# Cutting one weight load into 112, 8 and 8 partitions, so that the first eight DMA engines carry two rows more than the last eight

## The chip, the cores and the metric

The kernel runs on one core of one Trainium2 chip. Times are device microseconds of one execution; the shorter the better. A profiled execution gives a span (first to last instruction), about 1.8 us shorter than the time of the same run. Each run carries a state, slow when it took over 1.5% more than the fastest run of the same kernel.

## The reference, cut to what matters

Attention over pooled keys and values (batch 8, 8 heads, 576 positions, 64 dimensions) gives `x` of 4608 x 512. A soft mixture of 8 experts follows, 4 slots for each: 32 slots are weighted sums of all rows of `x`, each expert runs two dense layers on its slots, and each row of the output is a weighted sum of all slots.

```python
logits = x @ phi
d = exp(logits - logits.max(0)); d /= d.sum(0) + 1e-09
slot_input = (d.T @ x).reshape(E, S_per_e, D)
for e in range(E):
    h = np.maximum(slot_input[e] @ w1[e], 0.0)     # w1[e]: 512 x 1024 float32
    slot_out[e] = h @ w2[e]                        # w2[e]: 1024 x 512 float32
c = exp(logits - logits.max(1)); c /= c.sum(1) + 1e-09
return c @ slot_out
```

The inputs are 62 MB of float32 and the output 9.4 MB. The slots need all rows of `x`, and the output needs all slots.

## The kernel before

All inputs except `phi` are loaded by GpSimd (POOL), whose transfers convert float32 to bfloat16 on the way: first q, k and v in four pairs of batches, then `w1` of the eight experts, then `w2`. Each of these transfers covers 128 partitions. The last `w2` loads are cut by columns, so that the first half of the output columns can start before the rest has landed.

```python
    w1_sb = persist.tile([128, E, DJ, F], BF)

    def load_w1(e):
        nc.gpsimd.dma_start(out=w1_sb[:, e], in_=moe_w1[e].rearrange("(p j) f -> p j f", j=DJ))
    ...
    for pair in range(1, NP):
        ...                                   # k, q and v of the pair
        if pair == NP - 2:
            load_w1(0)
    for e in range(1, E):
        load_w1(e)
    load_w2(range(4), big, "big")
    ...
    for c in range(2):
        second(E - 2, c)                      # matmuls of expert 6 on column half c
        if c == 0:
            warm(6, junk)                     # filler matmuls that keep PE's clock up
        second(E - 1, c)                      # expert 7: waits for the last weights of half c
        slots_out(c)
        for g in range(NHALF):
            output(g, halves[c])
```

The softmax here doesn't subtract the row's maximum and nothing guards it: scores larger than these inputs give would overflow.

## Time and profile before

| | before |
|---|---|
| time, median of the first 6 runs | 178.92 us (177.95 to 179.39) |
| span of the profiled run | 176.2 us (time 178.02) |
| DMA queue 0 (all loads but `phi`), share of 16 engines | 86.6% |
| last weights of the first column half land | 146.76 us |
| last output lands | 174.56 us |

The page's table of 40 slices (each 4.4 us) has these rows for DMA; a digit is a tenth of the 16 engines' time, and below it stand the GB/s:

```profile
DMA  4999999999999999999999999999999999999995
GB/s 71 211 220 209 221 211 213 221 213 219 211 220 215 217 213 219 213 210 218 221 214 210 218 219 216 212 218 216 216 212 216 206 196 146 316 362 423 419 417 208
```

The engines are at least 90% busy from the second slice to the last but one. The loads count by what they write (bfloat16), so 215 GB/s written is 430 GB/s read. The queues of the same page (packets, MB, share of the engines' time):

```profile
q0 software_dynamic: 6768, 30.93, 86.6%
q1 hardware_dynamic: 3872, 9.50, 13.9%
q8 instruction: 11, 0.18, 0.4%
q14 instruction: 3, 0.02, 0.0%
```

Queue 1 carries the output and `phi`. Queue 8: eleven packets of 16 KB with instructions, 0.4% of the engines.

The chain of waits in order of time (start us, length us, what) around the end of the loads:

```profile
76.68 39.03 DMA w_big<-in_moe_w_dram
...
116.28 30.48 DMA w_xs<-in_moe_w_dram
146.76 0.04 issue
146.81 0.43 PE so_ps_2181 L447 x8
```

And PE's own timeline of these microseconds (start, length, what; in brackets how long it was idle before, and for what):

```profile
141.44 2.79 PE L112 MATMUL junk<-zeros 128*128 128x512 bf16 x7 [0.33 <-issue]
144.16 0.40 PE L447 MATMUL so_ps_2181<-w_xs,hT 128*32 128x256 bf16 x8
144.49 1.47 PE L112 MATMUL junk<-zeros 128*128 128x512 bf16 x6
146.81 0.40 PE L447 MATMUL so_ps_2181<-w_xs,hT 128*32 128x256 bf16 x8 [0.84 <-DMA w_xs<-in_moe_w_dram]
```

PE is done with everything else, fillers included, 0.84 us before the last weights come. The landing at 146.76 starts the outputs, and those are limited by DMA as well: 1 MB each 2.5 us to the end. So what moves this landing should move the time.

A landing is the sixteenth and last of the DMA engines' reports. The trace has all 16 times of each load. For the load that PE waits for here they are, in us behind the first of them (worked out from the trace's records, as all plain fences below):

```
0.00 0.18 0.35 0.38 0.58 0.70 0.85 1.11 1.24 1.33 1.40 1.61 2.03 2.54 2.55 2.64
```

The first engine was through 2.64 us before the last, and on average they were through 1.42 us before it: that is what a perfect balance could win here.

### The profile page before, as it was taken

Reading aid. Unit: us, or ns where it says so; the run is one execution under the profiler, and the core shown is the slowest. Engines: PE = TensorE matmul, PEld = TensorE weight load, DVE = VectorE, ACT = ScalarE, POOL = GpSimd, SP = SyncE. Lnnn points to the kernel's source line nnn. Section 1 sums busy time; section 2 is a strip of 40 time slices with the busy share of each in tenths; the row PEclk is TensorE's granted clock in tenths of the full one; section 3 lists DMA queues with packets and bytes.
Section 4 is the critical chain, followed back from the end, with each engine's and each line's share of the span. In section 5 each row is a group of like instructions: output and inputs, shape, how many; then the busy total and the mean of one; then the engine's idle time right before and its main releaser. Section 6 shows DMA issues by size and latency. Waiting matters only on the chain.

```text
span 176.2 us, 3523 instructions
## 1 busy us (share of the span) xinstructions
PE 134.0 (76%) x1467; PEld 84.2 (48%) x1469; DVE 90.7 (51%) x252; ACT 79.8 (45%) x146; POOL 18.5 (11%) x37
## 2 busy tenths in 40 slices
PE   7993999899999999999999869997422295787000
PEld 2363478557866678656755536356211132322000
DVE  5402602577777878778787696436000004899000
ACT  3022359697946978469798401120000003799000
POOL 6000100121001610111111001121200000000000
PEclk9999579999999999999999965999555569999655
DMA  4999999999999999999999999999999999999995
GB/s 71 211 220 209 221 211 213 221 213 219 211 220 215 217 213 219 213 210 218 221 214 210 218 219 216 212 218 216 216 212 216 206 196 146 316 362 423 419 417 208
DMA packets 10654, 40.64 MB, mean 231 GB/s; under 512 B 784, under 2 KB 6288, under 8 KB 6544
## 3 DMA queue, kind: packets, MB, share of 16 engines
q0 software_dynamic: 6768, 30.93, 86.6%
q1 hardware_dynamic: 3872, 9.50, 13.9%
q8 instruction: 11, 0.18, 0.4%
q14 instruction: 3, 0.02, 0.0%
HBM read 61.93 MB, written 9.44 MB: 405 GB/s over the span
## 4 chain that ended last, share of the span: by engine, by line
DMA 68%; PE 15%; ACT 6%; issue 2%; DVE 1%; POOL 0%; POOLq 0%; DVEq 0%
DMA w_big<-in_moe_w_dram 22%; DMA q_sb<-in_q_dram 18%; DMA w_xs<-in_moe_w_dram 17%; DMA v_sb<-in_v_dram 11%; PE f_ps L462 3%; PE q_ps L193 3%; PE pool_ps L179 3%; ACT w_sb L464 2%; PE sc L248 2%; PE G_ps L277 1%; PE u_ps L260 1%; PE fold_ps L204 1%; ACT ex_332 L249 1%; PE lg_ps L271 1%; DVE so L451 1%
## 5 line engine op out<-in xcount | busy, mean ns | idle before, releaser
L266 DVE TENSOR_TENSOR xs<-u_ps,rec 128x384 bf16<-128x384 f32 x72 | 39.4, 552 | 1.6
L248 PE MATMUL sc<-qT,kp 64*72 64x288 bf16 x128 | 22.9, 308 | 0.8 <-ACT ex_1633 L249 0.4
L265 DVE RECIPROCAL rec<-u_ps 128x4 f32<-128x4 f32 x72 | 12.5, 176 | 16.4 <-PE u_ps L260 16.1
L199 DVE COPY qT<-q_ps 128x768 bf16<-128x768 bf16 x16 | 8.8, 552 | 14.7 <-PE q_ps L193 14.6
L193 PE MATMUL q_ps<-ident,q_sb 128*128 128x128 bf16 x144 | 12.2, 229 | 4.4 <-DMA q_sb<-in_q_dram 3.9
L462 PE MATMUL f_ps<-so,cT 128*128 128x512 bf16 (+1 forms) x46 | 11.0, 331 | 3.5 <-DVE so L451 1.2
L464 ACT ACTIVATE o_sb_2311<-f_ps,recR 128x256 f32<-128x256 f32 x1 | 0.5, 474 | 29.1 <-PE f_ps L462 29.1
L451 DVE TENSOR_SCALAR so<-so_ps_2181,recC 128x256 bf16<-128x256 f32 x1 | 0.5, 484 | 23.9 <-PE so_ps_2181 L447 23.9
L248 PEld LDWEIGHTS <-kp 64*72 64x72 bf16 x128 | 8.7, 107 | 8.0 <-issue 2.5
L193 PEld LDWEIGHTS <-q_sb 128*128 128x128 bf16 x144 | 9.1, 102 | 6.4 <-DMA q_sb<-in_q_dram 4.8
L447 PEld LDWEIGHTS <-hT 128*32 128x32 bf16 x128 | 4.2, 118 | 16.4 <-issue 15.8
L112 PEld LDWEIGHTS <-zeros 128*128 128x128 bf16 x51 | 5.7, 119 | 9.8 <-issue 6.1
L182 ACT CAST kpar<-pool_ps 128x512 bf16<-128x512 f32 (+1 forms) x12 | 5.5, 485 | 10.6 <-PE pool_ps L179 10.5
L197 ACT COPY qT<-q_ps 128x768 bf16<-128x768 bf16 x8 | 6.4, 797 | 8.6 <-PE q_ps L193 8.6
L179 PE MATMUL pool_ps<-pmat,v_sb 128*128 128x128 bf16 x144 | 10.2, 227 | 0.0
L277 PE MATMUL G_ps<-xs,ee 128*128 128x512 bf16 x36 | 9.7, 405 | 0.4 <-ACT ee L272 0.4
L179 PE MATMUL pool_ps<-pmat,k_sb 128*128 128x128 bf16 x144 | 9.7, 219 | 0.1
L179 PEld LDWEIGHTS <-v_sb 128*128 128x128 bf16 x144 | 8.8, 102 | 0.8 <-issue 0.2
L462 PEld LDWEIGHTS <-cT 128*128 128x128 bf16 x46 | 4.3, 96 | 10.0 <-issue 7.6
L179 PEld LDWEIGHTS <-k_sb 128*128 128x128 bf16 x144 | 8.5, 98 | 0.8 <-issue 0.2
L466 DVE TENSOR_SCALAR w_sb<-f_ps,recR 128x512 f32<-128x512 f32 x12 | 8.3, 746 | 0.0
L464 ACT ACTIVATE w_sb<-f_ps,recR 128x512 f32<-128x512 f32 x12 | 7.7, 684 | 0.6
(165 smaller groups left out, 236.9 us busy)
## 6 DMA issues: line engine op xcount, KB each, us to landing
w_sb<-in_moe_w_dram POOLq DMA_DIRECT2D x8, 1024.0 KB, 34.6
out_dram<-w_sb SPq DMA_DIRECT2D x6, 1024.0 KB, 8.5
k_sb<-in_k_dram POOLq DMA_DIRECT2D x4, 1152.0 KB, 19.8
q_sb<-in_q_dram POOLq DMA_DIRECT2D x4, 1152.0 KB, 18.3
v_sb<-in_v_dram POOLq DMA_DIRECT2D x4, 1152.0 KB, 18.1
w_big<-in_moe_w_dram POOLq DMA_DIRECT2D x4, 1024.0 KB, 39.0
w_qT<-in_moe_w_dram POOLq DMA_DIRECT2D x2, 1024.0 KB, 39.0
w_xs<-in_moe_w_dram POOLq DMA_DIRECT2D x2, 512.0 KB, 27.5
```

The lines of the kernel that those rows point to most:

```text
L112: nc.tensor.matmul(out=ps, lhsT=zeros[:, 0:128], rhs=zeros, start=True, stop=True)
L179: nc.tensor.matmul(out=ps[:, r].rearrange("p n i -> p (n i)"), lhsT=src[:, tt:tt + 2, :].rearrange("p t d -> p (t d)"), rhs=pmat, start=(t ...
L193: nc.tensor.transpose(out=ps[:, t].rearrange("p n i -> p (n i)"), in_=q_sb[pair][:, tt:tt + 2, :].rearrange("p t d -> p (t d)"), identity= ...
L197: nc.scalar.copy(out=dst, in_=ps)
L199: nc.vector.tensor_copy(out=dst, in_=ps)
L248: nc.tensor.matmul(out=ps[:, r, 0:S // 2], lhsT=kp[pair][rows, n], rhs=qT[pair][rows, n], start=True, stop=True)
L265: nc.vector.reciprocal(out=rec, in_=ps[:, :, XW])
L266: nc.vector.tensor_tensor(out=xs[pair][:, t, qd * HQ:(qd + 1) * HQ, :], in0=ps[:, :, 0:XW], in1=rec.rearrange("p h -> p h ()").to_broadcas ...
L277: nc.tensor.matmul(out=ps, lhsT=ee[:, t].rearrange("p g s -> p (g s)"), rhs=x[:, t, :, 0:D], start=(t == 0), stop=(t == 8))
L462: nc.tensor.matmul(out=f_ps, lhsT=rows(r), rhs=so[:, cols], start=True, stop=True)
L464: nc.scalar.activation(out=o_sb[:, r], in_=f_ps, func=AF.Copy, scale=recR[:, g, r:r + 1])
L466: nc.vector.tensor_scalar(out=o_sb[:, r], in0=f_ps, scalar1=recR[:, g, r:r + 1], scalar2=None, op0=ALU.mult)
```

## The change

It cuts the load of expert 3's `w1` (1 MB) into three. A transfer of 112 partitions gives each of the 16 engines 7 rows (a row is 16 KB read and 8 KB written); each transfer of 8 partitions gives one row to each of the first 8 engines. So 9 rows go to the first eight and 7 to the last eight in place of 8 and 8. The intent is to take work from engines that finish late.

```diff
-    def load_w1(e):
-        nc.gpsimd.dma_start(out=w1_sb[:, e], in_=moe_w1[e].rearrange("(p j) f -> p j f", j=DJ))
+    def load_w1(e, cuts=()):
+        for p0, p1 in zip((0,) + cuts, cuts + (128,)):
+            nc.gpsimd.dma_start(out=w1_sb[p0:p1, e],
+                                in_=moe_w1[e, p0 * DJ:p1 * DJ].rearrange("(p j) f -> p j f", j=DJ))
 ...
     for e in range(1, E):
-        load_w1(e)
+        load_w1(e, cuts=(112, 120) if e == 3 else ())
```

## The prediction

> **What bounds the kernel now.** The load stream does. The 40-slice table has the DMA row at 9 from the second slice to the last but one, at a steady 206 to 221 GB/s until about 147 us; the chain of waits is 68% DMA. In time order that chain goes v_sb landing (76.2 us), w_big landing (115.7), w_xs landing (146.76), then the last `so_ps` matmuls, and outputs until 174.6. The output stage is DMA-bound too: from 150.1 us its transfers land back to back, 1 MB each 2.5 us. So the time is roughly "when the last weights land on the slowest DMA engine" plus a fixed tail.
>
> **What the packets show.** In the trace's packet records every w1 row (16 KB read, 8 KB written) takes 625 ns and the next starts 607 ns later, so every DMA engine runs at one fixed rate. Sixteen sequences of packets can be followed; they drift apart only at start-up and where a 16 KB instruction packet cuts in (queue 8, eleven of them). Each costs its engine 0.88 to 0.96 us, ten before 141 us. The Trainium skill ("Runtime: NRT & Kernel Launch", Instruction fetch mechanics) gives such refills 16 KiB blocks and calls the cost "mostly hidden"; the size agrees, but here every one delays loads. They hit only eight of the sixteen engines, two of these twice. By the 26th load (last landing 140.0 us) the eight are 1.08 to 2.62 us behind the foremost, the other eight 0 to 1.23. The last landing counts.
>
> **What the change does.** 112 partitions are 7 rows on each engine; two loads of 8 partitions are one row each. The Trainium skill ("DMA: Bandwidth & Descriptors", Why a DMA increments its semaphore by 16 and not by 1) allows such a transfer either on the first engines, or on 8 consecutive ones from a moving cursor. With the title's word for it, engines 0 to 7 get 9 rows and 8 to 15 get 7: plus and minus one row, 0.607 us. Added: two issues on POOL (0.53 us each; POOL is 11% busy) and two semaphore packets per engine (21 ns each). Semaphores rotate by eight, so a few weight loads are issued later (the first w2 load near 86 us, not 76), but at least four full loads remain queued, some 20 us: no starvation.
>
> **On the critical path.** If the eight refill engines are 8 to 15, which I think is the intent but can't see (engines aren't numbered in the trace), the slowest finishes 0.607 - 0.042 = 0.57 us earlier and all later steps move by that: the landing at 146.76 goes to about 146.2, the span 176.2 to about 175.6. If they are 0 to 7, it is 0.65 us slower. If the cursor alternates, nothing.
>
> **Predicted:** 178.4 us, 8 in 10 between 177.6 and 179.2; faster by over 2%: 0.01, within 2%: 0.98, slower: 0.01. The runs before spread over 1.4 us.
>
> **Signs.** Right: the landing spread of the last loads falls from 2.6 to about 2.0 us; the load after the split has eight engines 1.2 us nearer the others; the `so` wait ends near 146.2; DMA share and bytes unchanged; outputs still 2.5 us per MB. Wrong: the spread grows to 3.2 (wrong half) or stays (cursor); the 112-partition load runs slower than 7 x 0.607 us; POOL's later issues leave the DMA row below 9 around 85 to 95 us; instruction packets land on other engines.

## The result, and the profile after

The changed kernel took 178.29 us (median of 10 runs, 177.47 to 178.97), the kernel before 178.32 us (20 runs, 177.95 to 179.39). The ratio is 0.9986, with a 95% interval of 0.9960 to 1.0012. Ratios here are the mean time of one kernel's runs over that of the other's of the same rounds, so not quite the ratio of the medians. By this run alone it is the same time.

The times fall in two groups: five runs from 177.47 to 177.98 and five from 178.60 to 178.97. The profile belongs to the first group (177.81 us, span 176.0). The rows and queues that answer to those shown before:

```profile
DMA  4999999999999999999999999999999999999994
GB/s 69 205 220 214 220 215 212 219 212 222 209 222 214 218 214 216 216 211 218 216 218 210 216 218 220 208 216 214 222 214 212 210 193 160 330 361 424 417 424 188
...
q0 software_dynamic: 6816, 30.94, 86.7%
q1 hardware_dynamic: 3872, 9.50, 13.9%
q8 instruction: 11, 0.18, 0.4%
q14 instruction: 3, 0.02, 0.0%
```

The cut load in the list of DMA issues (KB each, median us from issue to landing):

```profile
w_sb<-in_moe_w_dram POOLq DMA_DIRECT2D x1, 896.0 KB, 27.8
w_sb<-in_moe_w_dram POOLq DMA_DIRECT2D x2, 64.0 KB, 27.3
```

Bytes and shares are unchanged. The two issues more don't starve the engines: the DMA row stays at 9, and the first `w2` load is issued at 87.0 us in place of 76.7 while others are still queued. The last weights of the first column half land at 146.27 us, 0.49 us earlier; the 16 landings spread over 2.28 us in place of 2.64. PE's timeline there:

```profile
140.95 3.19 PE L114 MATMUL junk<-zeros 128*128 128x512 bf16 x7 [0.33 <-issue]
144.08 0.62 PE L449 MATMUL so_ps_2183<-w_xs,hT 128*32 128x256 bf16 x8
144.62 1.94 PE L114 MATMUL junk<-zeros 128*128 128x512 bf16 x6
146.49 0.40 PE L449 MATMUL so_ps_2183<-w_xs,hT 128*32 128x256 bf16 x8
```

There is no bracket behind the last line: PE did not wait for the weights. The fillers ran at half clock until 145.6 us (the six took 1.94 us, not 1.47), and PE came to the weights 0.22 us after their landing. So of 0.49 us gained by the loads, 0.32 us were left when PE started (146.81 to 146.49), and 0.32 us at the end (the last output landed at 174.24 in place of 174.56). In this profile the mechanism works as predicted, a little smaller. What the profile of one run does not explain is the second group of times.

### The profile page after: what moved, and what is told of

It is laid out like the page before. It is cut to its first block, busy times and chain, and to the rows that moved or that the text cites. A ratio compares the mean times of both kernels' runs of the same rounds, so it can differ in the third digit from the quotient of the medians.

```text
span 176.0 us, 3529 instructions
## 1 busy us (share of the span) xinstructions
PE 140.0 (80%) x1467; PEld 88.0 (50%) x1469; DVE 90.9 (52%) x252; ACT 80.5 (46%) x146; POOL 19.7 (11%) x39
## 4 chain that ended last, share of the span: by engine, by line
PE 45%; DMA 34%; ACT 10%; issue 2%; DVE 1%; POOLq 0%; ACTq 0%; DVEq 0%
DMA w_qT<-in_moe_w_dram 18%; DMA q_sb<-in_q_dram 11%; PE sc L250 9%; PE pool_ps L181 8%; PE u_ps L262 7%; DMA k_sb<-in_k_dram 5%; PE q_ps L195 5%; PE G_ps L279 4%; PE f_ps L464 3%; PE junk L114 3%; ACT w_sb L466 2%; PE lg_ps L273 2%; PE fold_ps L206 2%; ACT ex_1634 L251 1%; ACT ex_1635 L251 1%
## 5 line engine op out<-in xcount | busy, mean ns | idle before, releaser
L250 PE MATMUL sc<-qT,kp 64*72 64x288 bf16 x128 | 24.7, 332 | 0.6 <-ACT ex_1635 L251 0.4
L195 PE MATMUL q_ps<-ident,q_sb 128*128 128x128 bf16 x144 | 14.2, 254 | 5.2 <-DMA q_sb<-in_q_dram 4.8
L195 PEld LDWEIGHTS <-q_sb 128*128 128x128 bf16 x144 | 10.8, 115 | 7.4 <-DMA q_sb<-in_q_dram 5.1
L279 PE MATMUL G_ps<-xs,ee 128*128 128x512 bf16 x36 | 11.2, 453 | 0.4 <-ACT ee L274 0.4
L114 PE MATMUL junk<-zeros 128*128 128x512 bf16 x25 | 7.9, 473 | 0.3 <-issue 0.3
```

The source lines that it names most:

```text
L114: nc.tensor.matmul(out=ps, lhsT=zeros[:, 0:128], rhs=zeros, start=True, stop=True)
L195: nc.tensor.transpose(out=ps[:, t].rearrange("p n i -> p (n i)"), in_=q_sb[pair][:, tt:tt + 2, :].rearrange("p t d -> p (t d)"), identity= ...
L250: nc.tensor.matmul(out=ps[:, r, 0:S // 2], lhsT=kp[pair][rows, n], rhs=qT[pair][rows, n], start=True, stop=True)
L279: nc.tensor.matmul(out=ps, lhsT=ee[:, t].rearrange("p g s -> p (g s)"), rhs=x[:, t, :, 0:D], start=(t == 0), stop=(t == 8))
```

## The experiments

The theories: **A**, the engine that finishes last sets the time, and only the shift of rows between engines matters. **B**, cutting and issuing more transfers itself moves the time. **C**, late landings are hidden. **D**, there is no gain, only noise. Others came up on the way. All kernels that are timed by the ratio here were run in five rounds beside the kernel before on the same chip; all outputs were correct.

### e1: a cut without a shift

```diff
-        load_w1(e, cuts=(112, 120) if e == 3 else ())
+        load_w1(e, cuts=(112,) if e == 3 else ())
```

> Expert 3's load is cut into 112 and 16 partitions, so every DMA engine still gets 8 rows: a cut without a shift. Theory A (only the shift of rows between engines matters): landings as in the kernel before, last weights of the first column half near 146.8 us with a spread of about 2.6 us, time ratio to before 1.000. Rival B (cutting and issuing more transfers itself moves the time, for instance through the later issues on POOL): ratio moves as in the changed kernel, about 0.998.

Ratio 0.9999 (0.9976 to 1.0022). The last landing was at 146.69 us with a spread of 2.66. These are the landings that theory A forecast. The ratio alone does not exclude B, whose 0.998 lies in the interval, and this kernel issues one transfer more where the change issues two; what speaks against B is that the landing did not move by 0.5 us.

### e2: two rows moved

```diff
-        load_w1(e, cuts=(112, 120) if e == 3 else ())
+        load_w1(e, cuts=(96, 104, 112, 120) if e == 3 else ())
```

> Expert 3 in 96 + 4 x 8 partitions: 10 rows on the first eight engines, 6 on the others, a shift of two rows (1.21 us). Theory A (time follows the engine that finishes last): the first eight, up to 1.23 us behind the foremost before, become the last; the last landing is about 0.1 us earlier than before and about 0.4 us later than with one row; spread over 2.4 us; ratio about 0.999 to 1.000. Rival B (every row taken off the slow engines gains): ratio about 0.994, last landing near 145.6.

Ratio 1.0060 (1.0031 to 1.0090), last landing 147.19 us, spread 3.63. More of the same is worse, against rival B; but it is 0.6% worse than before, and theory A with all visited engines in the last half had said no worse than before. Here my picture of who is late was incomplete. (In this profile some 45 packets of the cut load were also stretched; see "What stays open".)

### e3: four rows moved

```diff
-        load_w1(e, cuts=(112, 120) if e == 3 else ())
+        load_w1(e, cuts=(112, 120) if e >= 4 else ())
```

> Experts 4 to 7 each cut as in the change: four rows moved, 2.4 us. Theory A: the first eight engines now finish last, 1.23 + 2.43 + 0.17 - 2.62 = 1.2 us later than the last ones before; last critical landing near 148.0, spread near 5 us, ratio about 1.007. Rival C (a late landing is hidden by PE, which is itself late, or by the output stage): ratio stays within 0.2% of 1.

Ratio 1.0075 (1.0052 to 1.0098), as expected. In the profiled run, the slowest of the six (180.21 us), the last landing was at 149.22 us and the spread 7.13 us, both more than expected (148.0 and 5), and PE waited for the landing (chain of waits):

```profile
121.48 27.73 DMA w_xs<-in_moe_w_dram
...
149.26 0.43 PE so_ps L449 x8
```

So late landings are not hidden; C falls. The 16 landings fall in two groups of eight, which show who got the rows:

```
0.00 0.61 0.99 1.08 1.08 1.14 1.18 1.81 | 4.60 4.75 4.95 5.00 5.29 5.75 6.85 7.13
```

The right group is the first eight engines with their extra rows. Two of them stand 1.1 us and more behind the rest of their group. If the instruction packets hit only the last eight, nothing should set these two apart.

### Who is hit: the instruction packets go round a fixed ring

The packet records don't name engines. But a row takes 625 ns and the next starts 607 ns after it, to the nanosecond, so a sequence of packets can be followed from row to row. A 16 KB packet on queue 8 shows as a gap of 0.88 to 0.96 us in exactly one sequence. Each sequence also shows whether it carried 7 + 1 + 1 rows of the cut load or only 7; the former are the first eight engines in the sense of the title, the latter the last eight. Here are the start times of these packets and, in brackets, their durations in ns:

```
before          20.7(935) 33.1(975) 44.6(975) 54.1(962) 66.3(893) 74.6(892) 85.8(949) 97.2(945) 113.5(935) 123.4(975) 144.2(975)
changed         22.8(935) 32.9(974) 50.1(974) 59.6(961) 70.7(893) 79.4(893) 91.0(1024) 102.1(945) 120.9(936) 131.8(974) 143.5(975)
e3 (4 rows)     21.8(893) 32.3(893) 49.4(949) 59.1(945) 70.1(936) 78.9(974) 90.5(975) 101.6(961) 120.7(893) 131.9(893) 146.2(948)
e4 (changed)    22.3(961) 32.6(893) 50.9(893) 61.7(948) 73.0(945) 82.1(936) 93.4(975) 104.6(974) 121.9(961) 132.1(893) 144.4(893)
```

But for one (1024), the durations repeat in a fixed order: 935, 975, 975, 961, 893, 893, 948, 945, and from the start again. I call these places 1 to 8. Each place is one engine: the ninth packet hits the sequence that the first one hit. What differs from run to run is the place at which the ring starts: place 1 in the first two, place 5 in e3, place 4 in e4. Eleven packets come before the last landing (the eleventh near 144 us), so three engines are hit twice: the starting place and the two after it.

In the profile of the changed kernel, and again in those of e6 and e7 below, the sequences that carry the extra rows include the engines of places 5 and 6, and those of the other six places carry 7 rows. So six of the ring's engines are among the last eight, but two are among the first eight. I call it theory **E** that these two spoil the gain when they are hit twice. In e3 the ring started at place 5: both were hit twice, on top of four extra rows, and they are the two at 6.85 and 7.13.

The engine of place 4 stands out for another reason: it is already 0.9 to 1.5 us behind the foremost at its first load, in each profile where I looked (about 0.9 in the first, 1.04 in e12 below). A second engine of the last half starts about as late (in e6 9.65 us for its first 8 rows, against 9.70 for place 4 and 8.69 for the foremost), but no instruction packet hits that one in e6 or e7.

### e4: the changed kernel once more

> The changed kernel once more, beside the doses and with more rounds. Theory A: ratio 0.997 to 0.999, last critical landing about 0.5 us earlier than in the kernel before. Rival D (the 0.14% was noise and there is no gain at all): ratio 1.000 and over as often as under.

Ratio 0.9980 (0.9960 to 1.0001). The profiled run took 178.81 us and belongs to the slower group of times: last landing at 147.45, 1.18 us later than in the first profile of the same kernel. Its ring started at place 4.

### e5: the extra rows on engines that the ring may not visit

Theory E says that the two visited engines among the first eight spoil the gain when they are hit twice. From the ring's order I guessed that they are engines 6 and 7, so this kernel gives the extra rows to engines 0 to 5.

```diff
-        load_w1(e, cuts=(112, 120) if e == 3 else ())
+        load_w1(e, cuts=(112, 118, 124) if e == 3 else ())
```

> Expert 3 in 112 + 6 + 6 + 4 partitions: engines 0 to 3 get 9 + 1 = 10 rows, 4 and 5 nine, 6 to 15 seven. Theory E (from four traces: the eight engines that instruction packets visit in turn are six of the last eight and two of the first eight; whichever is visited twice is last; my estimate is that the two are 6 and 7): the extra rows now miss every visited engine, so the last landing is about 0.57 us earlier than before wherever the turn starts, ratio about 0.997, no upper group of runs near 178.8. Rival F (the two are others, say 0 and 1, or extra rows on the first half are harmless whoever is visited): if 0 and 1, some runs are over 1 us slower than before and the ratio is 1.000 or above.

Ratio 0.9988 (0.9963 to 1.0013), times 177.51 to 178.39: the group above 178.5 is missing, but in six runs that says little (the changed kernel had one such run of six in e4 and in e6), and the lower times are not better than those of the changed kernel. The profile, with the ring at place 4, has its last landing at 146.87 us and took 178.08 us. That is earlier than the changed kernel ever was with this start (147.20 to 147.45, below), which fits theory E. That the two are engines 6 and 7 is not shown: in this profile many packets of the cut load are stretched, and the sequences can't be told apart well enough.

### e6: the changed kernel a third time

> The changed kernel a third time, as the partner of the other two. Theory E: two groups of times about 1.2 us apart, 177.5 to 178.0 where the twice-visited engines are all in the last half, 178.6 to 179.0 where one of the first half is visited twice; ratio to before 0.997 to 1.000; the profile's time belongs to the group that its instruction packets say. Rival G (the two groups come from PE's clock): the group follows the granted clock around 140 to 147 us and not the engines.

Ratio 0.9972 (0.9948 to 0.9996). Times 177.49 to 177.79, and one of 178.61. The profiled run took 177.49 us; its ring started at place 7, and the engines hit twice (places 7, 8 and 1) are all in the last half. The last landing was at 146.12 us, and PE was waiting for it:

```profile
144.08 1.47 PE L114 MATMUL junk<-zeros 128*128 128x512 bf16 x6
146.16 0.40 PE L449 MATMUL so_ps<-w_xs,hT 128*32 128x256 bf16 x8 [0.61 <-DMA w_xs<-in_moe_w_dram]
```

The run to compare it with is e1, which has 8 rows everywhere and whose ring also started at place 7: 146.69 us. The change gained 0.57 us there, the predicted size. (e1 is the kernel before with one cut more; and each side is one profile.)

### e7: without the fillers

```diff
-        if e == E - 3:
-            warm(8, junk)
 ...
-        if c == 0:
-            warm(6, junk)
```

> The changed kernel without the 14 filler matmuls before the last weights. In its first profile PE began the last so matmuls 0.22 us after the landing (before: 0.05), because the fillers ran at half clock. Theory H (that is where part of the gain went): 0.1 to 0.2 us faster than the changed kernel, PE waits for the last landing in every profile. Theory E alone: same as the changed kernel, or slower by what a cold PE clock costs in the output stage.

Ratio 1.0055 (1.0032 to 1.0077): slower, theory H falls as a remedy. The landing was at 146.74 us here. The ring started at place 2 and hit place 4 a second time at 142.8 us: the spread was 2.00 us one load earlier and 2.74 at this landing. PE waited 2.98 us for it, but then everything that PE feeds was slow. The stretches of the two runs side by side (PE, PEld, DVE, ACT and POOL busy; granted PE clock, DMA share, GB/s), first e6, which has the fillers:

```profile
148.00:152.00 4.00, 2.80 (x28) 1.41 (x28) 3.19 (x9) 2.65 (x7) 0.00 (x0) 1.00 0.90 251
152.00:158.00 6.00, 5.04 (x21) 1.85 (x20) 5.92 (x11) 5.48 (x11) 0.00 (x0) 1.00 1.01 356
```

and e7, without them:

```profile
148.00:152.00 4.00, 3.71 (x26) 1.59 (x25) 2.50 (x6) 2.27 (x5) 0.00 (x0) 0.50 0.65 165
152.00:158.00 6.00, 5.35 (x18) 2.18 (x19) 4.79 (x9) 3.99 (x8) 0.00 (x0) 0.58 0.95 319
```

The granted clock was 0.50 to 0.58 in place of 1.00, the first outputs came later, and DMA stood partly idle (0.65 of its time in place of 0.90). The fillers cost up to 0.3 us where they run at half clock (0.29 in e9 below), and are worth keeping.

### e8: three more instruction packets (failed)

```diff
         for c in range(2):
             second(e, c)
+        for _ in range(64):
+            nc.tensor.matmul(out=junk[:, 0:1], lhsT=zeros[:, 0:128], rhs=zeros[:, 0:1], start=True, stop=True)
         if e == E - 3:
```

> The kernel before with 384 one-column matmuls in PE's waits for w2 (768 instructions more, three 16 KB instruction packets), about 2 us in each wait of 3.8. Theory A/E (instruction packets delay the engine that they hit by about 0.93 us and the last engine sets the time): 14 packets on queue 8 in place of 11, five engines hit twice before the last landing in place of two or three, last landing later by 0 to 0.6 us, ratio 1.001 to 1.004, never faster. Rival I (instruction packets cost nothing at the end): ratio 1.000, landing spread unchanged at 2.6 us.

Ratio 1.0187 (1.0131 to 1.0244), from two runs (180.56 and 182.68 us); the other four, up to 188.77, were slow, and so was the profile. The verdict on the time is therefore unclear. It does not test what it was made for. There were 14 packets, but the attention part had ended late in this run, the one-column matmuls no longer fitted into PE's waits, and PE became the limit: the last weights landed at 146.77 us as ever, PE reached them at 157.54. PE also stood still three times in the middle of the added matmuls, in the wait list of PE between 125 and 160 us:

```profile
PE junk L475 <- issue: 4.0, 3, 1.7
```

Each of these stops follows an instruction packet (138.0, 144.2, 149.5 us), so a refill may also stop PE itself. That the added packets delay the end through a DMA engine is not shown.

### e9, e10, e11 and e12: more looks

The changed kernel three times and the kernel before once, one profile each; the kernel before took 178.59 us in an unprofiled run beside them.

> The changed kernel, one look. Theory E: the eight visited engines are taken in a fixed order whose start differs from run to run, and the fourth and fifth places of one turn (recognised by a delay of 0.876 us each) are in the first eight, which now carry an extra row. If one of these two is visited twice before the last landing, last critical landing at 147.0 or later and a time of 178.5 or more; if not, landing at 146.1 to 146.4 and a time under 178.1. Rival G (PE's clock makes the groups): no such tie.

> As the run before it, another look: the same two-way forecast from its own instruction packets (one of the two 0.876 us engines visited twice: 147.0 or later and 178.5 or more; neither: 146.1 to 146.4 and under 178.1).

> As the two runs before it, a third look, same two-way forecast.

> The kernel before, one more look. Theory E: eight rows everywhere, so it doesn't matter which engines are visited twice: last critical landing 146.5 to 147.0, spread about 2.6 us, time 177.9 to 178.6.

All four rings started at place 4. The changed kernel landed at 147.35, 147.20 and 147.33 us and took 178.97, 178.56 and 178.68 us: the forecast for "one of the two visited twice" came true three times. The granted clock does not sort them (rival G): it was full from 144.2 us in e10, earlier than in the first profile (145.6), and e10 was 0.75 us slower than that run. The clock does add to one of them: in e9 the fillers ran at half clock until 146.8 us and PE came 0.29 us after the landing.

The forecast for e12 was wrong: the kernel before landed at 147.28 us, not by 147.0, with a spread of 3.33, and took 178.82 us. The engine that was last is that of place 4: it starts 1.04 us late and was hit at 22.0 and 122.0 us. So the kernel before has a slow case too. Its time holds something more: from PE's start on the last weights to the last output it took 28.02 us, against 27.73 to 27.77 us in the first two profiles and in all from e1 to e11 but e7 and e8. The granted clock was at half from 150.3 to 157.2 us in e12, which may be why; so the landings of this row compare better than the times. PE waited for the landing in both kernels, as in the timeline of e10:

```profile
147.24 0.40 PE L449 MATMUL so_ps<-w_xs,hT 128*32 128x256 bf16 x8 [0.86 <-DMA w_xs<-in_moe_w_dram]
```

and in that of e12:

```profile
147.32 0.40 PE L447 MATMUL so_ps<-w_xs,hT 128*32 128x256 bf16 x8 [1.02 <-DMA w_xs<-in_moe_w_dram]
```

The profiles to compare, by where the ring starts (one for each entry, so the 0.25 us between the four of place 4 is a measure of what one profile can say):

```
ring starts at   rows 8 and 8 (before, e1)      rows 9 and 7 (changed)                       difference of landings
place 1          146.76  (time 178.02)          146.27  (177.81)                              -0.49
place 7          146.69  (177.93, e1)           146.12  (177.49, e6)                          -0.57
place 4          147.28  (178.82, e12)          147.45 147.35 147.20 147.33  (178.56-178.97)  +0.05 (mean)
```

The last line can be worked out from e12 alone. These are its 16 landings of the load that PE waits for, the first at 143.95 us:

```
0.00 0.20 0.35 0.69 0.73 0.92 0.97 1.37 1.41 1.42 1.48 1.64 1.73 2.44 2.72 3.33
```

The last one, 3.33, is place 4, in the last half: the change takes a row (0.607 us) from it and adds four small packets, which together delay an engine by 21 ns (e6, e7), and that leaves about 2.75. The one before it, 2.72, is new there: three loads earlier no engine stood between 1.78 and 2.43. It is the one that was hit at 144.2 us, and by its duration that is place 6, in the first half. The change gives it a row and two small packets, 0.65 us. It then stands at 3.37, and 143.95 + 3.37 = 147.32. The four measured ones have a mean of 147.33. This is an estimate that agrees, made after the result.

**What stays open.** Why the ring starts where it does is not known; the timed rounds have no profile, so how often each start occurs there is not known either, and that the two groups of times are these starts is shown by six profiles of the changed kernel, not by the rounds. In six of the ten profiles of kernels with shifted rows, among them all five with the start at place 4, the packets of the cut load were stretched: some 15 to 45 packets by up to 0.47 us, together 1.5 to 4.6 us, thus 0.09 to 0.29 us for each engine on average. In the kernel before and in e1 this did not happen (one or two packets). Its cause is not known, and it may take part in the missing gain at place 4. It does not decide the landing by itself: e5 and e4, both with the start at place 4, had about as much of it (2.6 and 2.9 us in all), and e5 landed 0.58 us earlier. The first runs of the kernel before reach 179.39 us, more than any start that was profiled; these are not explained.

## Why the prediction was right or wrong

The time, 178.29 us, is within 0.11 us of the predicted 178.4, and "within 2%" came true. That closeness is partly luck: 178.4 is 0.5 us under the 178.92 of the first six runs of the kernel before, but over the twenty runs that median is 178.32, and no gain at all would have hit as well. What tests the mechanism is the landings. Point by point:

- **What bounds the kernel: right.** The last landing moves the end one for one (0.32 us at PE, 0.32 us at the last output; e3's profile 2.46 us later than before at the landing, 177.03 - 174.56 = 2.47 us at the end; 27.73 to 27.77 us from PE's start on the last weights to the last output in eleven profiles).
- **Rows at a fixed rate, the shift is one row: right.** With the start at place 7 the landing gained 0.57 us, as predicted. One term was too large: the small packets delay an engine that loses a row by 0.021 us (e6, e7), not by 0.042, so the sum should have been 0.59; the measured 0.49 and 0.57 are too few to tell.
- **"If the eight refill engines are 8 to 15": this step failed in part.** Six are; two are among the first eight and now carry an extra row. The prediction took the two engines hit twice in one profile as if they were always the same; the runs showed a ring that starts at different places. With the start at place 4 the gain is nil (0.05 us the wrong way), and its estimate from the kernel before fits.
- **"The slowest finishes 0.57 us earlier": right for two of the three starts compared** (0.49 and 0.57). The third has no gain. Each is one profile against one (four against one in the third). Over the three timed batches, the changed kernel had a mean of 178.07 us (22 runs) and the kernel before 178.39 (42 runs), a gain of 0.32 us; the three ratios are 0.9986, 0.9980 and 0.9972. The last alone excludes 1. So a gain of about 0.2% is likely, a little over half of what the sum said; how the starts mix to this figure is not shown.
- **All of the landing's gain reaches the end: not quite.** In the first profile 0.17 us were lost because PE's fillers ran at half clock.
- **The spread falls to about 2.0 us:** it fell to 2.28 and 2.22; with the start at place 4 it was 2.62 to 3.41, and 2.74 with place 2 (e7).
- **A moving cursor for the transfers of 8: no.** Both went to the same eight engines (the sequences with 7 + 1 + 1 rows; the two groups of eight in e3). The Trainium skill ("DMA: Bandwidth & Descriptors", Why a DMA increments its semaphore by 16 and not by 1) allows for both; the trace decides.
- **No starvation by POOL's later issues: right** (87.0 us for the first `w2` load, DMA row at 9 throughout).

## What to carry to other kernels

Where a kernel waits for a long stream of loads, look at the 16 landings of the load that it waits for, not at the mean DMA share: the distance from their mean to the last one (1.4 of the 2.6 us spread here) is time that balancing can win, and a cut at a partition count that fills only some engines is a cheap way to move it, one row at a time. Take more than one profile before you decide which engines are late: who was late here depended on where a ring of instruction packets started, and a fixed shift won half a microsecond in one case and nothing in another. A cut alone cost nothing that five rounds could show (e1, within 0.24%), but an overdone shift costs: four rows, 2.4 us, made the kernel 0.75% slower, about 1.3 us (e3).

## What the Trainium skill lacked or had wrong

- "Runtime: NRT & Kernel Launch", Instruction fetch mechanics, calls the cost of crossing a 16 KiB boundary "mostly hidden". The block size agrees (16,384 bytes in a packet). But in a kernel limited by loads each refill delays one DMA engine by 0.88 to 0.96 us, and the loads end with the last engine.
- No page that I read says which DMA engines the refills use. Here eleven refills go round eight of the sixteen in a fixed order (durations 935, 975, 975, 961, 893, 893, 948, 945 ns), six of them in the last half and two in the first, starting at places 1, 2, 4, 5, 7 or 8 in different runs.
- "DMA: Bandwidth & Descriptors", Latency and other measured facts, has engines 7 and 15 as usually slower, with ring contention as a guess. The trace does not number engines; the late ones here were those hit by refills, and two that were late from their first load on (0.96 and 1.01 us behind the foremost in e6).
- "DMA: Bandwidth & Descriptors", Why a DMA increments its semaphore by 16 and not by 1: that all 16 engines report for any shape agrees (16 landings more for each 8-partition transfer). The section does not say how many small packets an engine without data gets, or what they cost it: the records have 24 small packets for such a transfer, 8 + 2 x 8 (e5: 80 for transfers of 6, 6 and 4 partitions), and two such transfers together delayed an engine without data by 21 ns (e6, e7).
- The same section gives a moving cursor for transfers that use fewer than 16 engines, with an exception for some copies. Both transfers of 8 partitions filled the same eight engines in the profiles whose sequences can be followed (the first, e6 and e7), and all eight such transfers did in e3.
